# Attention and gated MLP on one core: a floor on the size of a dense phase, maxima closed by reductions, a normalization on ACT, and output tiles fetched two ahead

## The chip, the cores and the metric

The kernel runs on one core of one Trainium2 chip. The metric is device time in microseconds, the median of several runs. The kernel before has a median of 2049.7 us over three runs (2048.86 to 2051.69). Engines: PE is the matrix engine (PEld its weight load), DVE the vector engine, ACT the scalar engine, POOL GpSimd; SP issues nearly all DMAs.

## The reference

Input x has S = 2048 rows of D = 512 values. It is layer-normalized once, and two branches of the result are added to x:

```python
xn = layernorm(x)                                        # 2048 x 512
q, k, v = split(xn @ wqkv)                               # 32 heads of 16
A = concat_heads(softmax(q @ k.T / 4) @ v) @ wo          # attention
z = gelu(xn @ w_in)                                      # 2048 x 1792
z1, z2 = z[:, :896], layernorm(z[:, 896:])
g = w_sp @ z2 + b_sp[:, None]                            # 2048 x 2048 by 2048 x 896
out = x + A + (z1 * g) @ w_out
```

## The kernel before

The order of the instructions of each engine is written out by hand: a Python loop, which runs when the kernel is built, emits everything, and each engine then executes its own list in order. Two kinds of work share PE.

The first is attention. Two heads at a time (16 pairs), 4 chunks of 512 queries, 16 key tiles: 1024 steps. A step of the scores (`scores`, line 800) is a pair of matmuls into a PSUM tile `st`, which ACT turns into exp values `pf` (`exp`, line 814). The row maxima that the softmax subtracts come from another product of the same size: `max_mm` (line 556) writes a tile `mx`, `max_red` (line 566) reduces it on DVE. `st` and `mx` take turns in one ring of three PSUM tiles. `pv` (line 788) multiplies two steps of `pf` with v into `o`, eight small matmuls. `max_mm` runs 27 steps ahead of `scores`. After each 16 steps `max_fin` (line 574) closes a chunk: it negates the maxima, splits them into a rounded part and the rest (lines 581, 583, 584), transposes them (586), and two sets of DMAs bring them as additional rows into the operand of the scores.

The second is dense work, a `queue` of generators: the q and k projections (`qk_rest`), the second half of the first MLP product with its GELU and normalization (`z2_all`, `z2_norm`), its first half (`z1_all`), the product along the sequence (`spatial`), the last MLP product (`mlp_out`), the attention's output (`attn_out`). Each float32 product is three matmuls of rounded parts (`mm3`, line 164), called a triple here; after each triple the generator yields its cost in ns (650, or 570 in `z2_all`). An accumulator (`dpsum`, one PSUM bank) takes 4 triples in `qk`, `z2p`, `z1p` and `ao`, 16 in `sp`, 7 in `mo`.

The loop (line 832) goes by halves; two halves are a round of three steps. The first half emits st, mx, st and one or two `pv`; the second emits mx, st, mx and then a dense phase. A budget, `credit`, grows each round by three steps' share of the dense work still to do, spread to step 925 (`DENSE`). The phase goes on while the budget is positive:

```python
while credit > 0 and queue and not pause and not drain:
```

`drain` ends a phase at an accumulator's last triple (a yield with a fraction), because the bank must be emptied first; a yield that is not positive sets a pause, used at the start of a stage (-3) and where weights are missing (-1.5).

Weights are loaded by `prepare` (line 194): DMA into one of three raw buffers, then POOL rounds and splits them (`end`). As soon as `end` has been emitted the weight stands in the dictionary that its user polls. Work of POOL is timed by a model of its own: `gps` adds a cost to `pool[0]`, `clock()` is 2.7 us per half, and `pool_done` lets a generator wait until the model says that POOL has finished. `z2_norm` runs beside the dense phases as a side generator: GELU on POOL and ACT, statistics on DVE, the inverse deviation on POOL (lines 362 to 368), the normalization on DVE (370), the split for the next product. `attn_out` fetches a tile's operands from DRAM with `fetch` one tile ahead (lines 662 to 669).

Of the kernel before, what the change touches and what calls it, by code (L numbers as in the profile page):

```python
# [39 lines left out]
def fused_block(ctx, tc, x, wqkv, wo, w_in, w_spT, b_sp, w_out, out):  # L40
# [56 lines left out]

    steady = []
    side = []

    def raw(t):
        return t.bitcast(F32) if t.dtype == F32R else t
# [47 lines left out]
    def hilo(nm):  # L150
        return big.tile([P, 2, 512], F32R, tag="hilo", name=nm, bufs=3)

    def dpsum(nm, tag="d"):
        return ps.tile([P, 512], F32, tag=tag, name=nm, bufs=1)

    def spsum(nm):
# [37 lines left out]
    def prepare(out, loads, freed=None):  # L194


        loads, flight = list(loads), []
        while loads or flight:
            if flight and now[0] >= flight[0][0]:
                _, k, l = flight.pop(0)  # L200
                out[k] = end(l)
                rawfree.append(pool[0])
            if loads and len(rawfree) > 0 and clock() >= rawfree[0] and (freed is None or freed and now[0] >= freed[0]):
                rawfree.pop(0)
                if freed:
                    freed.pop(0)
                k, *a = loads.pop(0)
                flight.append((now[0] + 2, k, begin(*a)))
            yield
# [72 lines left out]
    def qk_group(m, g, w, tags=("d",)):  # L282
        for a in range(2):
            if now[0] < -2 and m:
                tags = ("d", "o")
            acc = dpsum(f"qk{m}_{a}_{g}", tags[a % len(tags)])
            for c in range(ND):
                t = xnT[g, c]
                mm3(acc, w[a][:, 0, c * P:(c + 1) * P], w[a][:, 1, c * P:(c + 1) * P], t[:, 0, :], t[:, 1, :], c == 0, c == ND - 1)
                yield 650 + 0.5 * (c == ND - 1)  # L290
            if m == 0:
                run(qk_split(m, g, a, acc))
                yield 0
                continue
            raw_ = t512(f"qr{m}_{a}_{g}")
            act(raw_, acc, AF.Copy, 512)
            side.append(qk_split(m, g, a, raw_))
            yield 0
# [43 lines left out]
    def z2_norm(t, z):  # L342


        z = z[:, :FH]
        u = piece(f"z2u{t}").bitcast(F32).rearrange("p a b -> p (a b)")[:, :FH]
        yield
        gelu_in(z, u, FH)
        yield from pool_done()
        act(u, u, AF.Tanh, FH, scale=GC)  # L350
        act(u, u, AF.Identity, FH, bias=1.0)
        yield
        gps(0.0024 * FH).tensor_mul(z, z, u)
        yield from pool_done()
        st = sm.tile([P, 2, 6], F32, tag="zst", name=f"zst{t}", bufs=2)
        mv = sm.tile([P, 2], F32, tag="zmv", name=f"zmv{t}", bufs=2)
        rs = sm.tile([P, 3], F32, tag="zrs", name=f"zrs{t}", bufs=2)
        for j in range(2):
            dve(448).bn_stats(st[:, j, :], z[:, j * 448:(j + 1) * 448])
        dve(12).bn_aggr(mv, st)  # L360
        yield
        gps(0.2).tensor_scalar(rs[:, 0:1], mv[:, 1:2], 1.0, 4 * EPS, ALU.mult, ALU.add)
        gps(0.6).tensor_tensor(rs[:, 1:2], rs[:, 0:1], mhalf, ALU.pow)

        gps(0.3).tensor_mul(rs[:, 2:3], rs[:, 1:2], rs[:, 1:2])
        gps(0.3).tensor_mul(rs[:, 2:3], rs[:, 2:3], rs[:, 0:1])
        gps(0.3).tensor_scalar(rs[:, 2:3], rs[:, 2:3], -0.5, 1.5, ALU.mult, ALU.add)
        gps(0.3).tensor_mul(rs[:, 1:2], rs[:, 1:2], rs[:, 2:3])
        yield from pool_done()
        dve(FH, 2).tensor_scalar(z, z, mv[:, 0:1], rs[:, 1:2], ALU.subtract, ALU.mult)  # L370
        for j, (lo, w) in enumerate(((0, 512), (512, 384))):
            yield
            hl = hilo(f"z2hl{t}_{j}")
            act(hl[:, 0, :w], z[:, lo:lo + w], AF.Copy, w)
            yield
            gps(0.0025 * w).tensor_sub(hl[:, 1, :w], z[:, lo:lo + w], hl[:, 0, :w].bitcast(F32))
            for a in range(2):
                store(z2scr[:, lo // P:(lo + w) // P, a, t, :], hl[:, a, :w].rearrange("p (f q) -> p f q", q=P), 1 + a)

    def z2_all():  # L380
# [11 lines left out]
        for t in range(NT):  # L392
# [4 lines left out]
                bg.append(prepare(w1, [(f, f"w1_{f}", w_in[:, f * P:(f + 1) * P], D, ND) for f in range(NF)]))  # L397
            z = piece(f"z2_{t}").bitcast(F32).rearrange("p a b -> p (a b)")
            for j in range(2):
                acc = dpsum(f"z2p{t}_{j}")  # L400
                for c in range(ND):
                    sl = slice(c * P, (c + 1) * P)
                    mm3(acc[:, :448], xt[:, 0, sl], xt[:, 1, sl], ws[c, j][:, 0, :448], ws[c, j][:, 1, :448], c == 0, c == ND - 1)
                    yield 570 + 0.5 * (c == ND - 1)
                act(z[:, j * 448:(j + 1) * 448], acc[:, :448], AF.Copy, 448)
                if j:
                    side.append(z2_norm(t, z))
                yield 0
# [12 lines left out]
    def z1_all():  # L421
        fetch_xnT(0)
        yield -2.5
        for g in range(NG):
            for f in range(NF):
# [3 lines left out]
                    fetch_xnT(g + 1, 2)  # L429
                while f not in w1:  # L430
                    yield -1.5
                acc = dpsum(f"z1p{f}_{g}")
                w = w1[f]
                for c in range(ND):
                    t = xnT[g, c]
# [11 lines left out]
    def spatial():  # L447
# [18 lines left out]
        order = [(g, f) for g in range(NG) for f in range(NF)]  # L466
        for n, (g, f) in enumerate(order):
            load_z1(g, f)
            acc = dpsum(f"sp{g}_{f}")
            nc.tensor.matmul(acc, onesr, brow, start=True, stop=False)  # L470
            if f == NF - 1 and g + 1 < NG:
                load_b(g + 1)
# [28 lines left out]
    def mlp_out():  # L501
# [14 lines left out]
        for t in range(NT):  # L516
# [2 lines left out]
                nxt = load(t + 1)  # L519
            if t == NT - 3:  # L520
                bg.append(prepare(wo_, [(g, f"wo{g}", wo[g * P:(g + 1) * P, :], 512) for g in range(4)]))
            acc = dpsum(f"mo{t}")
            for f in range(NF):
                h, sl = hp[f // 4], slice((f % 4) * P, (f % 4 + 1) * P)
                mm3(acc, h[:, 0, sl], h[:, 1, sl], wout[f][:, 0, :], wout[f][:, 1, :], f == 0, f == NF - 1)
# [48 lines left out]
    def max_fin(i):  # L574
# [2 lines left out]
            return  # L577
        g = i // 16
        p, c = divmod(g, 4)
        mn = at.tile([P, 2, 4], F32, tag="mn", name=f"mn{g}", bufs=1)  # L580
        nc.vector.tensor_reduce(mn, mmax.pop(g), AX.X, ALU.max, negate=True)
        mr = mrow[:, 0:16].rearrange("p (j a t) -> p j a t", j=2, a=2)
        nc.vector.tensor_copy(mr[:, :, 0, :], mn)
        nc.vector.tensor_sub(mr[:, :, 1, :], mn, mr[:, :, 0, :].bitcast(F32))
        ms = at.tile([P, 32], F32, tag="ms", name=f"ms{g}", bufs=2)
        nc.vector.transpose(ms, mrow.bitcast(F32))
        load["D"] += 0.6
# [50 lines left out]
    def attn_out():  # L638
# [18 lines left out]
        for j in range(2):  # L657
# [1 line left out]
            gps(0.2).tensor_add(ones[:, 0, j * DH:(j + 1) * DH], a, b)  # L659
            a, b = (ident[:, 64 * j + 32 * r + DH:64 * j + 32 * r + DH + 1].to_broadcast([P, DH]) for r in range(2))  # L660
            gps(0.2).tensor_add(ones[:, 0, (2 + j) * DH:(3 + j) * DH], a, b)
        nxt = fetch(0)
        yield -3
        while len(wo_) < 4:
            yield -1.5
        for t in range(NT):
            op = nxt
            if t + 1 < NT:
                nxt = fetch(t + 1)
            while t // 4 not in lasthl:  # L670
                yield -1
            acc = dpsum(f"ao{t}")
            for g in groups:
                mm3(acc, op[:, 0, g, :], op[:, 1, g, :], wo_[g][:, 0, :], wo_[g][:, 1, :], g == 0, False)
                yield 650
# [55 lines left out]
    with tc.manual_schedule(engines=engines):  # L731
# [76 lines left out]
        N = len(order)  # L808
        sts, full = {}, {}
        credit = 0.0  # L810
        ready = rounds = 0
        ended = []

        def exp(n):
            pf = at.tile([P, 1024], F32, tag="pf", name=f"pf{n}", bufs=PF)
# [16 lines left out]
        for half in range(-2 * LEAD // 3, 2 * (N // 3 + 4)):  # L832
# [60 lines left out]
            if urgent and between and not drain and "ones" in sel:  # L893
                queue.insert(0, urgent.pop(0))
                pause = 0
            while credit > 0 and queue and not pause and not drain:
                cost = next(queue[0], None)
                if cost is None:
                    queue.pop(0)
                elif cost <= 0:  # L900
                    pause = -cost
                else:
                    drain = between = cost % 1 > 0
                    credit -= cost
                    todo -= cost
        while queue or urgent or bg or late or turn:
            now[0] += 1
            flush()
# [35 lines left out]
```

## Time and profile before

| | |
|---|---|
| median of three runs | 2049.7 us |
| the profiled execution's own time | 2054.62 us |
| its span, first to last instruction | 2052.8 us |
| PE busy | 1991.7 us, 97% |
| DVE busy | 1457.4 us, 71% |
| ACT busy | 1219.3 us, 59% |
| POOL busy | 517.0 us, 25% |
| mean granted clock of PE | 0.990 |

The rows of the trace that the prediction uses stand in a section below. In a row of the timeline the columns are start, duration, engine, line, operation, output and inputs, and in brackets how long the engine had been idle before it and what released it.

### The profile page before, as it was taken

Reading aid. Unit: us, or ns where it says so; the run is one execution under the profiler, and the core shown is the slowest. Engines: PE = TensorE matmul, PEld = TensorE weight load, DVE = VectorE, ACT = ScalarE, POOL = GpSimd, SP = SyncE. Lnnn points to the kernel's source line nnn. Section 1 sums busy time; section 2 is a strip of 40 time slices with the busy share of each in tenths; the row PEclk is TensorE's granted clock in tenths of the full one; section 3 lists DMA queues with packets and bytes.
Section 4 is the critical chain, followed back from the end, with each engine's and each line's share of the span. In section 5 each row is a group of like instructions: output and inputs, shape, how many; then the busy total and the mean of one; then the engine's idle time right before and its main releaser. Section 6 shows DMA issues by size and latency. Waiting matters only on the chain.

```text
span 2052.8 us, 30367 instructions
## 1 busy us (share of the span) xinstructions
PE 1991.7 (97%) x11548; PEld 1030.6 (50%) x11548; DVE 1457.4 (71%) x1614; ACT 1219.3 (59%) x1396; POOL 517.0 (25%) x560
## 2 busy tenths in 40 slices
PE   7999999899999999999999999999999999999998
PEld 6764454454444445454444455545554454454442
DVE  5377788878777767776777777777777767766773
ACT  4346677676666655555555655555566655555555
POOL 2203267677344620005011320005001200011100
PEclk9999999999999999999999999999999999999999
DMA  9586253354434545354454745255364635353322
GB/s 323 189 317 200 93 137 106 92 127 141 129 105 131 153 152 135 99 150 155 113 143 138 203 142 133 91 129 181 108 161 142 172 123 154 97 167 102 103 80 96
DMA packets 233850, 293.05 MB, mean 143 GB/s; under 512 B 34656, under 2 KB 134688, under 8 KB 230824
## 3 DMA queue, kind: packets, MB, share of 16 engines
q1 hardware_dynamic: 229480, 281.07, 46.8%
q0 software_dynamic: 4224, 10.04, 1.3%
q8 instruction: 91, 1.49, 0.3%
q14 instruction: 55, 0.45, 0.1%
HBM read 189.06 MB, written 101.98 MB: 142 GB/s over the span
## 4 chain that ended last, share of the span: by engine, by line
PE 86%; DVE 8%; DMA 3%; ACT 1%; issue 1%; SPq 1%; POOL 0%; DVEq 0%; ACTq 0%; POOLq 0%
PE o L798 22%; PE mx L564 15%; PE st L805 14%; PE sp L165 6%; DVE mm L572 6%; PE sp L166 5%; PE sp L167 5%; PE mo L165 2%; PE z1p L165 1%; PE qk L165 1%; PE z2p L165 1%; PE mo L166 1%; PE mo L167 1%; PE qk L166 1%; PE qk L167 1%; PE z1p L166 1%
## 5 line engine op out<-in xcount | busy, mean ns | idle before, releaser
L572 DVE TENSOR_REDUCE mm<-mx 128x2 f32<-128x1024 f32 x1024 | 1218.2, 1221 | 498.8 <-PE mx L564 497.7
L57 ACT ACTIVATE pf<-st 128x1024 f32<-128x1024 f32 x1024 | 1017.7, 1024 | 716.8 <-PE st L805 696.4
L798 PE MATMUL o<-pf,vall 128*32 128x512 f32 x4096 | 518.0, 607 | 0.0
L805 PE MATMUL st<-qst,kst 50*128 50x512 f32 x2048 | 450.3, 437 | 25.9 <-DVE mm L572 23.5
L564 PE MATMUL mx<-kst,qst 48*128 48x512 f32 x2048 | 459.1, 446 | 7.2 <-DVE mm L572 3.3
L564 PEld LDWEIGHTS mx<-kst,qst 48*128 48x128 f32 x2048 | 193.0, 186 | 354.2 <-ACT pf L57 288.7
L805 PEld LDWEIGHTS st<-qst,kst 50*128 50x128 f32 x2048 | 193.5, 186 | 195.5 <-DVE mm L572 91.9
L798 PEld LDWEIGHTS o<-pf,vall 128*32 128x32 f32 x4096 | 99.0, 109 | 221.7 <-issue 220.0
L165 PE MATMUL sp<-wsp,zs 128*128 128x512 f32 x448 | 191.1, 427 | 1.4 <-POOL wsp L190 1.4
L166 PE MATMUL sp<-wsp,zs 128*128 128x512 f32 x448 | 176.4, 394 | 0.0
L167 PE MATMUL sp<-wsp,zs 128*128 128x512 f32 x448 | 175.7, 392 | 0.6 <-POOL wsp L191 0.6
L165 PEld LDWEIGHTS sp<-wsp,zs 128*128 128x128 f32 x448 | 83.9, 187 | 56.2 <-issue 40.1
L190 POOL CAST wsp<-wsp_0r 128x512 fp32r<-128x512 f32 x4 | 2.5, 612 | 370.9 <-DMA wsp_0r<-in_w_spT 370.9
L167 PEld LDWEIGHTS sp<-wsp,zs 128*128 128x128 f32 x448 | 84.1, 188 | 20.5 <-POOL wsp L191 1.1
L166 PEld LDWEIGHTS sp<-wsp,zs 128*128 128x128 f32 x448 | 84.3, 188 | 13.3
L615 POOL TENSOR_TENSOR ob<-ob 128x512 f32<-128x512 f32 (+1 forms) x16 | 20.5, 1283 | 255.4 <-DMA ob<-escr 255.4
L620 POOL TENSOR_TENSOR ob<-ob 128x512 f32<-128x512 f32 (+1 forms) x16 | 20.6, 1288 | 162.4 <-DMA ob<-rscr 104.4
L165 PE MATMUL z2p<-w,xt 128*128 128x448 f32 x128 | 52.1, 407 | 0.0
L165 PE MATMUL mo<-wout,hp 128*128 128x512 f32 x112 | 48.5, 433 | 0.0
L190 POOL CAST wo<-wo0r 128x512 fp32r<-128x512 f32 x1 | 0.6, 612 | 188.8 <-DMA wo0r<-in_wo 188.8
L167 PE MATMUL z2p<-w,xt 128*128 128x448 f32 x128 | 47.6, 372 | 0.0
L166 PE MATMUL z2p<-w,xt 128*128 128x448 f32 x128 | 47.6, 372 | 0.0
(371 smaller groups left out, 1918.8 us busy)
## 6 DMA issues: line engine op xcount, KB each, us to landing
zs<-z2scr SPq DMA_DIRECT2D x112, 512.0 KB
escr<-e SPq DMA_DIRECT2D x60, 256.0 KB
hscr<-hhl SPq DMA_DIRECT2D x28, 512.0 KB
qst<-qscr SPq DMA_DIRECT2D x30, 384.0 KB
kst<-kscr SPq DMA_DIRECT2D x30, 384.0 KB
xscr<-xnT POOLq DMA_DIRECT2D x16, 512.0 KB, 5.9
qscr<-qkhl SPq DMA_DIRECT2D x16, 512.0 KB
kscr<-qkhl SPq DMA_DIRECT2D x16, 512.0 KB
```

The lines of the kernel that those rows point to most:

```text
L57: return nc.scalar.activation(out, in_, func, **kw)
L165: nc.tensor.matmul(acc, lh, rh, start=first, stop=False)
L166: nc.tensor.matmul(acc, ll, rh, start=False, stop=False)
L167: nc.tensor.matmul(acc, lh, rl, start=False, stop=last)
L190: gps(0.6).tensor_copy(t[:, 0, :n], rw[:, :n])
L564: nc.tensor.matmul(acc[:, j, :], qst[p % 2][rows, tt * P:(tt + 1) * P], kst[p % 2][rows, kc * 512:(kc + 1) * 512], start=True, stop=True)
L572: dve(1024).tensor_reduce(mmax[i // 16][:, :, t, kc], mstep.pop(i), AX.X, ALU.max)
L615: gps(1.3).tensor_add(both[rows, 0, :], both[rows, 0, :], both[rows, 1, :])
L620: gps(1.3).tensor_mul(both[rows, 0, :], both[rows, 0, :], both[rows, 2, :])
L798: nc.tensor.matmul(acc[cols:cols + VW, :], vpack(kt - 1 + r, 2 * p + j), pf[:, j * 512:(j + 1) * 512], start=(kt == 1), stop=(kt == NT - 1))
L805: nc.tensor.matmul(st[:, j, :], kst[p % 2][rows, kt * P:(kt + 1) * P], qst[p % 2][rows, c * 512:(c + 1) * 512], start=True, stop=True)
```

## The change

Four edits.

1. `dpsum` notes in `left` how many triples its accumulator takes, and each triple counts it down. The phase's condition becomes `go()`: the first triple needs a positive budget; the second is always taken; a third and further ones need a positive budget while more than two triples are left in the accumulator; with two left they need more than 650; with one left the triple is taken.
2. In `prepare` a weight enters the user's dictionary only when the model clock has passed POOL's end of its split (`made`).
3. `max_fin` closes a chunk with four `tensor_reduce`: the rounded negative maximum, the exact negative maximum, the rounded positive one, and the sum of the last two, which is the rest. Before, it was a `tensor_reduce`, a `tensor_copy` and a `tensor_sub`.
4. `z2_norm` works out -mean/deviation with two more small operations on POOL and normalizes on ACT (`Identity` with scale and bias) in place of DVE's `tensor_scalar`; `attn_out` fetches two tiles ahead in place of one.

```diff
@@ -97,6 +97,7 @@
     steady = []
     side = []
+    left = [0]
     def raw(t):
         return t.bitcast(F32) if t.dtype == F32R else t
@@ -150,7 +151,8 @@
     def hilo(nm):
         return big.tile([P, 2, 512], F32R, tag="hilo", name=nm, bufs=3)
-    def dpsum(nm, tag="d"):
+    def dpsum(nm, tag="d", n=1):
+        left[0] = n
         return ps.tile([P, 512], F32, tag=tag, name=nm, bufs=1)
     def spsum(nm):
@@ -194,11 +196,15 @@
     def prepare(out, loads, freed=None):
-        loads, flight = list(loads), []
-        while loads or flight:
+        loads, flight, made = list(loads), [], []
+        while loads or flight or made:
+            if made and clock() >= made[0][0]:
+                _, k, t = made.pop(0)
+                out[k] = t
             if flight and now[0] >= flight[0][0]:
                 _, k, l = flight.pop(0)
-                out[k] = end(l)
+                t = end(l)
+                made.append((pool[0], k, t))
                 rawfree.append(pool[0])
             if loads and len(rawfree) > 0 and clock() >= rawfree[0] and (freed is None or freed and now[0] >= freed[0]):
                 rawfree.pop(0)
@@ -283,7 +289,7 @@
         for a in range(2):
             if now[0] < -2 and m:
                 tags = ("d", "o")
-            acc = dpsum(f"qk{m}_{a}_{g}", tags[a % len(tags)])
+            acc = dpsum(f"qk{m}_{a}_{g}", tags[a % len(tags)], ND)
             for c in range(ND):
                 t = xnT[g, c]
                 mm3(acc, w[a][:, 0, c * P:(c + 1) * P], w[a][:, 1, c * P:(c + 1) * P], t[:, 0, :], t[:, 1, :], c == 0, c == ND - 1)
@@ -366,8 +372,10 @@
         gps(0.3).tensor_mul(rs[:, 2:3], rs[:, 2:3], rs[:, 0:1])
         gps(0.3).tensor_scalar(rs[:, 2:3], rs[:, 2:3], -0.5, 1.5, ALU.mult, ALU.add)
         gps(0.3).tensor_mul(rs[:, 1:2], rs[:, 1:2], rs[:, 2:3])
+        gps(0.3).tensor_mul(rs[:, 2:3], mv[:, 0:1], rs[:, 1:2])
+        gps(0.3).tensor_scalar(rs[:, 2:3], rs[:, 2:3], -1.0, 0.0, ALU.mult, ALU.add)
         yield from pool_done()
-        dve(FH, 2).tensor_scalar(z, z, mv[:, 0:1], rs[:, 1:2], ALU.subtract, ALU.mult)
+        act(z, z, AF.Identity, FH, bias=rs[:, 2:3], scale=rs[:, 1:2])
         for j, (lo, w) in enumerate(((0, 512), (512, 384))):
             yield
             hl = hilo(f"z2hl{t}_{j}")
@@ -397,7 +405,7 @@
                 bg.append(prepare(w1, [(f, f"w1_{f}", w_in[:, f * P:(f + 1) * P], D, ND) for f in range(NF)]))
             z = piece(f"z2_{t}").bitcast(F32).rearrange("p a b -> p (a b)")
             for j in range(2):
-                acc = dpsum(f"z2p{t}_{j}")
+                acc = dpsum(f"z2p{t}_{j}", n=ND)
                 for c in range(ND):
                     sl = slice(c * P, (c + 1) * P)
                     mm3(acc[:, :448], xt[:, 0, sl], xt[:, 1, sl], ws[c, j][:, 0, :448], ws[c, j][:, 1, :448], c == 0, c == ND - 1)
@@ -429,7 +437,7 @@
                     fetch_xnT(g + 1, 2)
                 while f not in w1:
                     yield -1.5
-                acc = dpsum(f"z1p{f}_{g}")
+                acc = dpsum(f"z1p{f}_{g}", n=ND)
                 w = w1[f]
                 for c in range(ND):
                     t = xnT[g, c]
@@ -466,7 +474,7 @@
         order = [(g, f) for g in range(NG) for f in range(NF)]
         for n, (g, f) in enumerate(order):
             load_z1(g, f)
-            acc = dpsum(f"sp{g}_{f}")
+            acc = dpsum(f"sp{g}_{f}", n=NT)
             nc.tensor.matmul(acc, onesr, brow, start=True, stop=False)
             if f == NF - 1 and g + 1 < NG:
                 load_b(g + 1)
@@ -519,7 +527,7 @@
                 nxt = load(t + 1)
             if t == NT - 3:
                 bg.append(prepare(wo_, [(g, f"wo{g}", wo[g * P:(g + 1) * P, :], 512) for g in range(4)]))
-            acc = dpsum(f"mo{t}")
+            acc = dpsum(f"mo{t}", n=NF)
             for f in range(NF):
                 h, sl = hp[f // 4], slice((f % 4) * P, (f % 4 + 1) * P)
                 mm3(acc, h[:, 0, sl], h[:, 1, sl], wout[f][:, 0, :], wout[f][:, 1, :], f == 0, f == NF - 1)
@@ -577,11 +585,16 @@
             return
         g = i // 16
         p, c = divmod(g, 4)
-        mn = at.tile([P, 2, 4], F32, tag="mn", name=f"mn{g}", bufs=1)
-        nc.vector.tensor_reduce(mn, mmax.pop(g), AX.X, ALU.max, negate=True)
+        mm = mmax.pop(g)
+        mn = at.tile([P, 2, 4, 2], F32, tag="mn", name=f"mn{g}", bufs=1)
         mr = mrow[:, 0:16].rearrange("p (j a t) -> p j a t", j=2, a=2)
-        nc.vector.tensor_copy(mr[:, :, 0, :], mn)
-        nc.vector.tensor_sub(mr[:, :, 1, :], mn, mr[:, :, 0, :].bitcast(F32))
+        nc.vector.tensor_reduce(mr[:, :, 0, :], mm, AX.X, ALU.max, negate=True)
+        nc.vector.tensor_reduce(mn[:, :, :, 0], mm, AX.X, ALU.max, negate=True)
+        nc.vector.tensor_reduce(mn.bitcast(F32R)[:, :, :, 1], mm, AX.X, ALU.max)
+        with nc.allow_low_precision(reason="the second of two parts, of which the first is exact"):
+            nc.vector.tensor_reduce(mr[:, :, 1, :], mn, AX.X, ALU.add)
         ms = at.tile([P, 32], F32, tag="ms", name=f"ms{g}", bufs=2)
         nc.vector.transpose(ms, mrow.bitcast(F32))
         load["D"] += 0.6
@@ -659,17 +672,17 @@
             gps(0.2).tensor_add(ones[:, 0, j * DH:(j + 1) * DH], a, b)
             a, b = (ident[:, 64 * j + 32 * r + DH:64 * j + 32 * r + DH + 1].to_broadcast([P, DH]) for r in range(2))
             gps(0.2).tensor_add(ones[:, 0, (2 + j) * DH:(3 + j) * DH], a, b)
-        nxt = fetch(0)
+        nxt = [fetch(0), fetch(1)]
         yield -3
         while len(wo_) < 4:
             yield -1.5
         for t in range(NT):
-            op = nxt
-            if t + 1 < NT:
-                nxt = fetch(t + 1)
+            op = nxt.pop(0)
+            if t + 2 < NT:
+                nxt.append(fetch(t + 2))
             while t // 4 not in lasthl:
                 yield -1
-            acc = dpsum(f"ao{t}")
+            acc = dpsum(f"ao{t}", n=4)
             for g in groups:
                 mm3(acc, op[:, 0, g, :], op[:, 1, g, :], wo_[g][:, 0, :], wo_[g][:, 1, :], g == 0, False)
                 yield 650
@@ -808,8 +821,16 @@
         N = len(order)
         sts, full = {}, {}
         credit = 0.0
+        took = 0
         ready = rounds = 0
         ended = []
+        def go():
+            if took == 0 or left[0] > 2 and took > 1:
+                return credit > 0
+            return left[0] == 1 or took == 1 or credit > 650
         def exp(n):
             pf = at.tile([P, 1024], F32, tag="pf", name=f"pf{n}", bufs=PF)
@@ -893,7 +914,8 @@
             if urgent and between and not drain and "ones" in sel:
                 queue.insert(0, urgent.pop(0))
                 pause = 0
-            while credit > 0 and queue and not pause and not drain:
+            took = 0
+            while queue and not pause and not drain and go():
                 cost = next(queue[0], None)
                 if cost is None:
                     queue.pop(0)
@@ -903,6 +925,8 @@
                     drain = between = cost % 1 > 0
                     credit -= cost
                     todo -= cost
+                    left[0] -= 1
+                    took += 1
         while queue or urgent or bg or late or turn:
             now[0] += 1
             flush()
```

## Rows read from the trace of the kernel before

**Rows 1.** The page, busy us and share of the span by engine.
```profile
PE 1991.7 (97%) x11548; PEld 1030.6 (50%) x11548; DVE 1457.4 (71%) x1614; ACT 1219.3 (59%) x1396; POOL 517.0 (25%) x560
```
**Rows 2.** Waits of PE's matmuls: us in total, times, longest.
```profile
PE st L805 <- DVE mm L572: 23.5, 56, 3.0
...
PE ao L165 <- DMA op<-oscr: 3.0, 2, 1.5
...
PE sp L165 <- POOL wsp L190: 1.4, 1, 1.4
```
**Rows 3.** Timeline, PE behind a phase of one triple.
```profile
513.65 0.50 PE L805 MATMUL st<-qst,kst 50*128 50x512 f32 x2
...
514.59 0.50 PE L805 MATMUL st<-qst,kst 50*128 50x512 f32 x2 [0.20 <-DVE mm L572]
```
**Rows 4.** Timeline, DVE in the same stretch.
```profile
512.19 3.48 DVE L572 TENSOR_REDUCE mm<-mx 128x2 f32<-128x1024 f32 x3
```
**Rows 5.** Windows of four rounds: start:end, us, busy us by engine, clock, DMA.
```profile
513.65:520.77 7.12, 6.92 (x41) 3.56 (x40) 5.06 (x5) 4.02 (x6) 3.96 (x4) 1.00 0.94 265
563.44:570.04 6.60, 6.60 (x41) 3.56 (x40) 5.03 (x9) 3.56 (x4) 2.77 (x3) 1.00 0.62 219
1043.49:1050.77 7.28, 7.07 (x42) 3.75 (x41) 5.97 (x8) 3.62 (x4) 1.28 (x1) 1.00 0.35 110
1241.47:1248.28 6.81, 6.81 (x42) 3.75 (x41) 5.54 (x10) 3.48 (x4) 0.00 (x0) 1.00 0.44 119
```
**Rows 6.** Timeline, PE, behind the first and the last of the 35 phases.
```profile
159.54 0.50 PE L805 MATMUL st<-qst,kst 50*128 50x512 f32 x2 [0.27 <-DVE mm L572]
...
1955.66 0.50 PE L805 MATMUL st<-qst,kst 50*128 50x512 f32 x2 [0.21 <-DVE mm L572]
```
**Rows 7.** Lines 581, 583, 584: duration ns min/median/max, first and last start, forms.
```profile
L581 DVE TENSOR_REDUCE mn<-mm x64: 169/177/190, 122.2 to 2001.3; 128x8 f32<-128x32 f32 x64
...
L583 DVE CAST mrow<-mn x64: 170/171/1857, 122.4 to 2001.5; 128x8 fp32r<-128x8 f32 x64
...
L584 DVE TENSOR_TENSOR mrow<-mn,mrow x64: 166/168/2000, 122.6 to 2001.7; 128x8 fp32r<-128x8 f32 x64
```
**Rows 8.** Timeline, one close of a chunk: POOL, DVE, then PE.
```profile
405.52 2.09 POOL L353 TENSOR_TENSOR z<-z,z2u 128x896 f32<-128x896 f32 x1
...
405.64 2.00 DVE L584 TENSOR_TENSOR mrow<-mn,mrow 128x8 fp32r<-128x8 f32 x1
...
409.05 0.80 PE L805 MATMUL st<-qst,kst 50*128 50x512 f32 x2 [3.02 <-DVE mm L572]
```
**Rows 9.** Windows of two rounds of the z2 stage.
```profile
374.05:383.49 9.44, 6.70 (x33) 2.13 (x33) 6.00 (x9) 5.27 (x6) 4.36 (x8) 0.82 0.40 114
...
409.05:419.12 10.07, 10.07 (x32) 5.61 (x33) 5.92 (x7) 5.18 (x6) 1.36 (x6) 0.50 0.55 139
```
**Rows 10.** Line 370; ACT on tiles of 896, by lines; the z2 stage (windows).
```profile
L370 DVE TENSOR_SCALAR z<-z,zmv,zrs x16: 705/1265/2461, 249.2 to 506.3; 128x896 f32<-128x896 f32 x16
...
L57 ACT ACTIVATE z2u<-z2u 128x896 f32<-128x896 f32 x29 | 27.7, 954 | 0.4
...
209.00:464.00 255.00, 241.84 (x1417) 127.51 (x1416) 202.04 (x218) 181.46 (x226) 158.04 (x170) 0.97 0.40 107
```
**Rows 11.** Timeline, POOL's last small operation of a z2 tile, DVE's normalization.
```profile
247.76 0.19 POOL L368 TENSOR_TENSOR zrs<-zrs 128x1 f32<-128x1 f32 x1
...
249.18 0.89 DVE L370 TENSOR_SCALAR z<-z,zmv,zrs 128x896 f32<-128x896 f32 x1
```
**Rows 12.** Timeline, PE at two tiles of the attention's output.
```profile
1892.53 0.47 PE L165 MATMUL ao<-wo,op 128*128 128x512 f32 x1 [1.45 <-DMA op<-oscr]
...
1920.25 0.47 PE L165 MATMUL ao<-wo,op 128*128 128x512 f32 x1 [1.55 <-DMA op<-oscr]
```
**Rows 13.** Windows: a round with no dense phase; start of the output stage.
```profile
707.03:711.41 4.38, 3.13 (x22) 1.13 (x22) 3.49 (x4) 3.71 (x6) 4.22 (x6) 1.00 0.66 152
...
1872.00:1881.00 9.00, 8.65 (x30) 5.10 (x32) 3.79 (x4) 3.89 (x5) 1.28 (x1) 0.62 0.64 189
```

## The prediction

> **What bounds the kernel now.** I read the page first: PE is busy 97% of the span, every other engine at most 71% [rows 1]. So only two things can help: less PE work, of which the change takes none away, or fewer holes and slow stretches of PE. Next the waits of PE's own matmuls: the largest entry, 23.5 us in 56 waits, is a score tile that waits for a DVE reduction; two waits for the output's operands come to 3.0 us [rows 2]. Then the timeline of PE, round by round. From the first score matmul of one round to that of the next, a round's length depends on two things alone in undisturbed places: whether it holds one or two emissions of `pv` (8 or 16 small matmuls), and the number of triples. With 16, an undisturbed round takes 6.60 us with 4 triples of z1, and 6.81 with 4 of sp and the bias matmul (second and fourth of [rows 5]). Of the 332 rounds from 149 to 1999 us, those that are longer than their like are of four kinds, and they follow here.
>
> **Phases of one triple (edit 1).** 41 rounds hold one triple: 10 in z2p, 9 in z1p, 9 in sp, 5 in mo, 4 each in qk and ao. The reason is the mechanism of the budget: 3 triples leave it below zero, the fourth of an accumulator comes a round later, alone, and then the accumulator ends the phase. In the ring of three PSUM tiles the second score tile of the next round takes the place of the second mx of the round before. DVE needs 3.48 us for its three reductions, from 512.19 to 515.67 in the case shown, the last of them for a later tile [rows 4]; with one triple between, PE is back at 513.65, and its second score tile starts only at 514.59, released by DVE [rows 3]. The round behind a single is then 7.12 against 6.60 in z1p and 7.28 against 6.81 in sp, with the same 16 small matmuls and the same triples [rows 5]: 0.52 and 0.47, taken as 0.5. Rounds behind a phase of two show no such excess, and the single rounds themselves are not longer than their one triple asks. Of the 41, four are followed by a round with no phase at the end of a stage, one by the last pair's sums and one by the disturbed round of the next part. The other 35 (the first and the last in [rows 6]) give 35 x 0.5 = 17 us.
>
> Does `go()` remove them? In accumulators of 4 the phase now has 4 triples where the budget is over 1950 (1790 in z2p, at 570 each) at its start, otherwise 2. Income is about 1850 per round, more than the 1300 of two triples, so no round goes empty for that, and the work done per round stays. In sp and mo the third triple goes by the old rule, a last one is always taken. A single is left only where a pause cuts a phase. Bounds: 12 (a third stay) to 20 (the 23.5 of [rows 2] less the 3.0 of [rows 8], which is of another kind). I take 17.
>
> **Chunks of maxima (edit 3).** Lines 583 and 584 take 0.17 us by the median and up to 1.86 and 2.00; line 581, a reduction, never more than 0.19 in 64 chunks [rows 7]. The long ones coincide with two-input operations of POOL: in the case shown POOL starts at 405.52 for 2.09, DVE's subtraction starts at 405.64 and ends with it, and the cast before it, 1.86 long, ended so with the POOL operation before. PE stands 3.02 us for the reductions behind, and restarts with matmuls of 0.80 in place of 0.50 [rows 8]: the granted clock is 0.50, the lower level of 1.2 GHz, for the whole round that follows, 10.07 us of PE work that would be about half at 2.4 GHz [rows 9]. Two places are like this, both in the z2 stage. The round at 374.05 is 9.44 us long with 6.70 of PE busy, so 2.7 idle, and its mean clock is 0.82, so 0.18 x 9.44 = 1.7 lost to the clock [rows 9]: 4.4. The idle 3.02 of [rows 8] ends the round before 409.05, and of the 10.07 behind it at most half, 5.0, is the clock's; I take 4.5, since other waits would have shown again. Sum 4.4 + 3.0 + 4.5 = 11.9.
>
> All four closing operations are now of the kind of line 581. The Trainium skill, SBUF — State Buffer, "Who interferes with whom", says it as a rule: a copy, a cast or a `tensor_scalar` can need the port pair that DVE shares with GpSimd, a subtraction with two SBUF inputs contends with its reads, a `tensor_reduce` never does. The trace agrees [rows 7]; by this rule each close stays under 1 us wherever POOL is, and all of the 11.9 could go. The Trainium skill also speaks against the edit: VectorE: DVE Perf Modes, "Rules for kernel authors", calls `tensor_reduce` the slowest DVE operation, always at the single rate, to be restructured on a hot path. By that page the edit would lose a little in each of 64 closes; the reduction of 32 values takes 7 ns more than the cast of 8 by the medians [rows 7], 64 x 4 x 7 ns = 2 us of DVE in all.
>
> The cost: one operation more per chunk, 0.18 plus a start of 0.03, 64 x 0.21 = 13 us of DVE work. DVE is idle 29% of the span [rows 1], so most of it is covered; where a round is short and holds a close, up to 0.2 shows. I charge 1 in all, with 0 and 13 as ends. In the two bad rounds DVE still has statistics and a close, so I count 11 of the 11.9 as gained (8 to 12).
>
> **Normalization on ACT (edit 4).** 16 operations of line 370 leave DVE, 0.71 to 2.46 us each, median 1.27 [rows 10], also stretched by POOL. ACT gets 16 of 0.95, by its other operations of 896 elements, 15 us; in the z2 stage (255 us) ACT goes from 181 to 196 busy, DVE from 202 to about 181 [rows 10]. POOL gets 16 x 2 operations of 0.19 plus gaps of 0.08, 9 us, behind which nothing of PE waits. What is queued behind the new ACT operation is the next exp, and behind that a score tile: if POOL is late, PE stands. Before, DVE found POOL's values ready by 1.2 us or more in each of the 16 tiles; the narrowest is that of [rows 11], and the two new operations need 0.56 of it. So: no new wait. The effect on PE is that of a few half microseconds in z2p rounds: between 4 gained and 3 lost, taken as 1 gained.
>
> **Output tiles two ahead (edit 4) and stage starts.** PE waits 1.45 and 1.55 for a tile of `op` [rows 12]: 3 us, which go if the fetch is one tile earlier, since a tile's four triples and what is between take over 5 us. More pieces of the ring of 20 are in use, at most 17 by my count (8 output tiles, 3 operands, 4 weights, 2 for the last pair), so no fetch waits for a piece. Each stage starts with rounds of no phase, 4.38 us with PE busy 3.13 in one, so 1.2 lost, and a slow clock behind them, 0.62 over 9 us at the output stage, 3.4 lost [rows 13]. They stay, as the pause of 3 stays; where the single ahead of them goes, the hole is smaller: 2 gained (0 to 8, four such stretches).
>
> **Weights flagged later (edit 2).** A weight is seen one half later, so a phase may be put off; on the other hand PE no longer stands for POOL's split. It did for 1.4 us in one wait [rows 2]. With 8 changes of weights (4 stages and the 4 columns of w_sp), I take 0, from 1 gained to 10 lost (8 rounds without a phase at 1.2, as that of [rows 13]).
>
> **Sum.** 17 + 11 + 1 + 3 + 2 - 1 = 33 us, of 2054.6 for the profiled execution: 2021.6. That execution is 4.9 us above the median of the runs, so the same gain from 2049.7 gives 2016.7: 2017 us.
>
> **Rivals.** (a) The loss behind singles isn't cured but moved: DVE's reductions set the pace over two rounds, and phases of two in place of three and one give the same waits in smaller parts. For it: DVE is at 71% [rows 1], and its three reductions alone are 3.5 us of each round [rows 4]. Against: rounds behind two triples show no excess. Time: 17 less gained, 2034. (b) The chunk closes still collide, or another DVE operation (the GELU's, line 340) meets POOL instead, and the low clock falls elsewhere: 11 less gained, 2028. (c) The weights' flag makes stages start late: 16 rounds without a phase at 1.2, 19 us: 2036. (d) Slower: ACT's normalization waits for POOL at the head of ACT's list, the exp behind it is late, and PE stands in each of the 16 z2 tiles as in the round at 374, 2.7 us [rows 9]; from 33/16 = 2.1 us per tile on the whole gain is gone; at 2.7 the time is 2017 + 43 = 2060. Against it stands the slack of [rows 11].
>
> **How the numbers follow.** The forecast has 0.70, (a) 0.10, (b) 0.11, (c) 0.04, (d) 0.05. All but (d) are faster by more than 0.2% (4 us, about what can be told from no change); for what I have not thought of I move 0.07 away: faster 0.88, same 0.06, slower 0.06. The low end takes nearly all bounds at their best, 20 + 12 + 4 + 3 + 5 = 44: 2005 or so. The high end takes in (a), (b) and (c): 2038.
>
> **What would show it.** In the trace after: no dense phase of one triple inside a stage, and the wait of `st` for `mm` under 6 us. The closing reductions all near 0.18 us. No stretch at the low clock between 370 and 420. No wait of `ao` for `op`. ACT never waiting for `zrs`. Wrong: PE's waits for DVE still near 20 us, a new entry of ACT waiting for POOL, or more rounds without a phase than six.

## The result, and the profile after

The changed kernel takes 2019.55 us (median of 4, 2015.84 to 2020.96), the kernel before 2049.82 beside it. The ratio is 0.9844 with a 95% interval of 0.9825 to 0.9862. In a later series it was 0.9829 (0.9815 to 0.9844). That is 32 to 35 us; 33 were forecast, and 2017.

The page of the changed kernel, busy us and share of the span (2016.4 us), to be compared with [rows 1]:

```profile
PE 1976.3 (98%) x11548; PEld 1027.4 (51%) x11548; DVE 1427.1 (71%) x1662; ACT 1229.9 (61%) x1412; POOL 518.2 (26%) x592
```

PE has the same 11548 matmuls and is 15 us less busy; the rest of the 36 us of span was idle. Read window by window, the time at a granted clock of 0.50 fell from 42.8 to 24.8 us, and half of that difference, 9, is about what the clock gave back (an estimate). The rounds behind a single triple also counted as busier, 6.92 us against 6.60 in [rows 5]. The waits of PE's matmuls, to be compared with [rows 2]:

```profile
PE st L818 <- DVE mm L580: 8.0, 18, 0.9
PE z1p L167 <- DMA xnT__4621<-xscr: 2.7, 1, 2.7
...
PE ao L167 <- DMA op<-oscr: 0.3, 1, 0.3
```

The score tile's wait for a reduction fell from 23.5 us in 56 places to 8.0 in 18, and the output's operands from 3.0 to 0.3. No round holds a single triple any more: the rounds of z1 now hold 4 or 2. Windows of three rounds, columns as in [rows 5]:

```profile
552.89:559.49 6.60, 6.60 (x42) 3.57 (x42) 4.59 (x5) 3.45 (x4) 3.32 (x4) 1.00 0.55 141
...
381.68:388.02 6.34, 5.59 (x35) 2.51 (x35) 3.45 (x4) 6.05 (x7) 5.37 (x5) 1.00 0.21 59
...
238.01:243.09 5.08, 5.08 (x37) 2.45 (x36) 3.00 (x3) 4.35 (x6) 2.21 (x2) 1.00 0.13 51
```

The first is the 4-triple round behind a phase of two: 6.60, PE without a hole, where the round behind a single took 7.12 in [rows 5]. The other two are rounds of two z2 triples with 16 small matmuls; behind a phase of four such a round is 5.08, behind a phase of two it can be 6.34. This is new, and is taken up below.

The four operations that close a chunk (minimum, median, maximum ns; the first of 64 and one case in order of time), against [rows 7] and [rows 8]:

```profile
L593 DVE TENSOR_REDUCE mrow<-mm x64: 174/177/189, 120.8 to 1965.3; 128x8 fp32r<-128x32 f32 x64
...
455.60 0.17 DVE L593 TENSOR_REDUCE mrow<-mm 128x8 fp32r<-128x32 f32 x1
455.70 0.18 DVE L594 TENSOR_REDUCE mn<-mm 128x8 f32<-128x32 f32 x1
455.79 0.18 DVE L595 TENSOR_REDUCE mn<-mm 128x8 fp32r<-128x32 f32 x1
456.00 0.17 DVE L597 TENSOR_REDUCE mrow<-mn 128x8 fp32r<-128x16 f32 x1
456.20 0.21 DVE L599 STREAM_TRANSPOSE ms<-mrow 128x32 f32<-128x32 f32 x1
```

Not one is stretched (the maxima of the other three are 180, 180 and 171 ns), and the first three, which don't depend on each other, start 0.10 apart. From the first start to the transposition it is 0.60 us for four operations; three took 0.62 at the first close of the kernel before, where nothing stretched them.

One stretch got no better, the start of z1. Timeline of PE, window of the round, and window of the slow clock:

```profile
465.31 0.47 PE L167 MATMUL z1p<-xnT__4621,w 128*128 128x512 f32 x1 [2.68 <-DMA xnT__4621<-xscr]
...
465.79:472.62 6.83, 6.39 (x17) 3.35 (x16) 0.00 (x0) 0.30 (x1) 4.93 (x4) 0.50 0.72 237
458.25:471.49 13.24, 9.83 (x41) 4.45 (x42) 4.57 (x4) 4.91 (x6) 11.88 (x14) 0.78 0.84 269
```

PE waits 2.68 us for a transfer and then works 6.83 us at a granted clock of 0.50, the 1.2 GHz level. This differs from run to run. In another profile of the same kernel, whose run took 2013.19 us, the only such stretch here is 3.41 us long and lies ahead of the start, at 456.12; behind the waits for the same transfers (0.91, 0.33 and 0.68) the clock is full. The kernel before had its own stretch there, 3.4 us from 470.4.

### The profile page after: what moved, and what is told of

Its sections match the earlier page's. It is cut to its first block, busy times and chain, and to the rows that moved or that the text cites. A ratio compares the mean times of both kernels' runs of the same rounds, so it can differ in the third digit from the quotient of the medians.

```text
span 2016.4 us, 30429 instructions
## 1 busy us (share of the span) xinstructions
PE 1976.3 (98%) x11548; PEld 1027.4 (51%) x11548; DVE 1427.1 (71%) x1662; ACT 1229.9 (61%) x1412; POOL 518.2 (26%) x592
## 5 line engine op out<-in xcount | busy, mean ns | idle before, releaser
L57 ACT ACTIVATE pf<-st 128x1024 f32<-128x1024 f32 x1024 | 1015.0, 1024 | 670.8 <-PE st L818 653.9
L811 PE MATMUL o<-pf,vall 128*32 128x512 f32 x4096 | 512.8, 602 | 0.0
```

Source lines behind the costliest of these rows:

```text
L57: return nc.scalar.activation(out, in_, func, **kw)
L811: nc.tensor.matmul(acc[cols:cols + VW, :], vpack(kt - 1 + r, 2 * p + j), pf[:, j * 512:(j + 1) * 512], start=(kt == 1), stop=(kt == NT - 1))
```

## Experiments

All were timed over five rounds, beside the kernel before on the same chip; so each has its own ratio, and differences between series go by the ratios. Two readings run through the expectations. By the additive theory each edit is worth its own term of the sum, whatever the others do; by coupling, two edits remove parts of the same stall, so their gains don't add up.

**Edit 1 alone.** The kernel before with `left`, `took` and `go()`:

```diff
-            while credit > 0 and queue and not pause and not drain:
+            took = 0
+            while queue and not pause and not drain and go():
```

> The kernel before with the floor of two triples alone (edit 1). Additive theory: the singles are worth 17 us by themselves, so about 2033 against 2050, and the stalls at the chunk closes near 374 and 405 with their low clock stay. Rival (coupling): both bad closes of the kernel before lie in rounds of a single triple; with two triples there PE has cover for the late reductions, so the closes no longer show and this edit alone gives 25 us or more, 2025 or less. Rival (a) of the prediction, the loss is only moved: under 8 us.

Measured: 2027.93, ratio 0.9893 (0.9878 to 0.9907), 22 us. That lies between the additive theory and coupling. One bad place of the z2 stage had gone and one was left, with the low clock behind it. DVE in that place:

```profile
362.25 2.00 DVE L372 TENSOR_SCALAR z<-z,zmv,zrs 128x896 f32<-128x896 f32 x1
364.17 1.21 DVE L574 TENSOR_REDUCE mm<-mx 128x2 f32<-128x1024 f32 x1
365.30 0.17 DVE L585 TENSOR_REDUCE mn<-mm 128x8 f32<-128x32 f32 x1
365.51 1.76 DVE L587 CAST mrow<-mn 128x8 fp32r<-128x8 f32 x1
367.31 1.21 DVE L588 TENSOR_TENSOR mrow<-mn,mrow 128x8 fp32r<-128x8 f32 x1
```

and PE behind it:

```profile
371.18 0.79 PE L566 MATMUL mx<-kst,qst 48*128 48x512 f32 x2 [2.48 <-DVE mm L574]
```

From 370.91 to 377.73 the granted clock is 0.50. The stall is a pile: a stretched normalization and a stretched close in one round. Two triples don't cover 5 us of them, and three didn't either. The same pile in the kernel before, DVE and then PE:

```profile
367.49 2.17 DVE L370 TENSOR_SCALAR z<-z,zmv,zrs 128x896 f32<-128x896 f32 x1
370.92 1.75 DVE L583 CAST mrow<-mn 128x8 fp32r<-128x8 f32 x1
372.71 1.22 DVE L584 TENSOR_TENSOR mrow<-mn,mrow 128x8 fp32r<-128x8 f32 x1
...
372.03 0.47 PE L165 MATMUL z2p<-w,xt 128*128 128x448 f32 x1
376.60 0.49 PE L564 MATMUL mx<-kst,qst 48*128 48x512 f32 x2 [2.04 <-DVE mm L572]
382.56 0.47 PE L165 MATMUL z2p<-w,xt 128*128 128x448 f32 x1
```

That both bad closes lie in rounds of a single triple, as the expectation has it, holds for the one at 405 alone. Here the close lies in a round of three triples, whose first matmul is the one at 372.03, and the single triple of the next round, at 382.56, comes behind the stall. The other bad place went with this edit, but not because two triples cover a long close there: the same close, now at 398.39, is hardly stretched (cast 0.46 and subtraction 0.17 us).

**Edit 3 alone.** The kernel before with the four reductions:

```diff
-        nc.vector.tensor_reduce(mn, mmax.pop(g), AX.X, ALU.max, negate=True)
...
-        nc.vector.tensor_copy(mr[:, :, 0, :], mn)
-        nc.vector.tensor_sub(mr[:, :, 1, :], mn, mr[:, :, 0, :].bitcast(F32))
+        nc.vector.tensor_reduce(mr[:, :, 0, :], mm, AX.X, ALU.max, negate=True)
+        nc.vector.tensor_reduce(mn[:, :, :, 0], mm, AX.X, ALU.max, negate=True)
+        nc.vector.tensor_reduce(mn.bitcast(F32R)[:, :, :, 1], mm, AX.X, ALU.max)
...
+            nc.vector.tensor_reduce(mr[:, :, 1, :], mn, AX.X, ALU.add)
```

> The kernel before with the chunk closed by four reductions alone (edit 3). Additive theory: 11 us, about 2039; the waits of st for mm stay near 17 us, since singles stay. Coupling: the same here, 8 to 12 us, since singles are still there to expose the closes. Rival (b), the closes still collide: 0 to 2 us.

Measured: 2040.76, ratio 0.9953 (0.9938 to 0.9968), 10 us, as both theories had it; that the closes still collide is refuted. From 370 to 420 the granted clock is 1.00. At the first bad place the normalization is still 2.16 us long, and behind it PE waits 0.25 us: without the stretched close the pile is too small to matter.

**Edits 1 and 3 together**, both diffs above:

> Edits 1 and 3 together on the kernel before, without the flag, the ACT normalization and the earlier fetch. Additive theory: 28 us, 2022. Coupling: about as much as edit 1 alone, plus 2 to 5: 2020 to 2025. In both the two waits of ao for op stay.

Measured: 2023.29, ratio 0.9874 (0.9858 to 0.9890), 26 us. Apart they are worth 22 and 10. So some 6 us are counted by both, though the intervals are wide against that. It fits the rows: of the 11.9 us that the prediction reads from [rows 8] and [rows 9], 7.5 belong to the place that edit 1 removes too, and the 4.4 of the place that it leaves are about what edit 3 adds on top of it, 4 (an estimate).

**Edit 1 undone in the changed kernel**, the first diff the other way:

> The changed kernel with the budget's old condition (edit 1 undone). Additive theory: 17 us slower than the changed kernel, about 2036, about 41 phases of one triple again and st waiting for mm about 20 us. Rival (a): under 8 us slower.

Measured: 2029.20, ratio 0.9901 (0.9886 to 0.9916), 12 to 15 us slower than the changed kernel in its two series; the additive 17 is just too much, rival (a)'s 8 too little. 40 phases of one triple are back, and with them the wait for DVE:

```profile
PE st L818 <- DVE mm L580: 19.4, 51, 0.9
```

**Is it DVE that a single phase waits for?** The same kernel, with each reduction of maxima over half its keys:

```diff
-            while queue and not pause and not drain and go():
+            while credit > 0 and queue and not pause and not drain:
...
-        dve(1024).tensor_reduce(mmax[i // 16][:, :, t, kc], mstep.pop(i), AX.X, ALU.max)
+        dve(1024).tensor_reduce(mmax[i // 16][:, :, t, kc], mstep.pop(i)[:, :, :256], AX.X, ALU.max)
```

> The budget's old condition, so some 40 phases of one triple, but each reduction of maxima reads 256 of its 512 keys (the maxima of the other half are left out of what softmax subtracts), so DVE's three reductions take about half of 3.5 us. Theory (a round behind a single waits for DVE's third reduction): the excess of 0.47 us of these rounds goes, and with it all of the 10 to 14 us that the old condition cost, so at most 2018. Rival (the excess belongs to PE itself, to the change between the forms of matmul or to the short phase): the excess stays near 0.4 and the time near 2029.

Measured: 1999.34, ratio 0.9764 (0.9751 to 0.9777). Windows of a single z1 round and the 4-triple round behind it, first with whole reductions, then with halved ones:

```profile
514.01:517.93 3.92, 3.92 (x24) 1.66 (x23) 3.14 (x4) 3.13 (x4) 0.32 (x1) 1.00 0.12 44
517.93:525.06 7.13, 6.86 (x41) 3.57 (x41) 5.67 (x10) 3.90 (x5) 2.99 (x3) 1.00 0.16 54
```

```profile
504.53:508.45 3.92, 3.92 (x24) 1.61 (x23) 2.68 (x4) 3.11 (x4) 0.32 (x1) 1.00 0.18 67
508.45:515.06 6.61, 6.61 (x42) 3.57 (x41) 3.21 (x9) 3.83 (x5) 2.95 (x3) 1.00 0.15 46
```

The single rounds are equal. Behind them it is 7.13 with 0.27 of PE not busy, and 6.61 with no hole. Nothing of PE's list differs. So the excess is the wait for DVE, and neither the short phase itself nor the change between forms of matmul costs anything here. The time fell by 28 us, twice what the old condition costs, so halving takes away more than the waits behind singles: the time at a granted clock of 0.50 also falls from 20.4 to 5.2 us in the two profiles.

**The changed kernel with halved reductions**, the second half of that diff:

> The changed kernel with the same halved reductions (half of the maxima left out). In the changed kernel the second of two rounds with two z2 triples is still 0.5 to 0.7 us too long. Theory: these wait for DVE, so they shorten to the length of their like, and with the stage starts' waits for DVE 5 to 8 us go: about 2010. Rival: they wait for ACT, whose work is unchanged here: within 3 us of the changed kernel, and the halved reductions with singles then are no slower than this kernel.

Measured: 2002.15, ratio 0.9780 (0.9767 to 0.9793), 10 to 13 us faster than the changed kernel, more than either theory had, and yet the z2 rounds did not shorten, which is what the rival said of them: the round that was 6.34 is 6.32. Its window, ACT and PE in it:

```profile
375.57:381.89 6.32, 5.32 (x35) 2.44 (x34) 2.45 (x5) 6.03 (x7) 5.36 (x5) 1.00 0.21 60
...
374.39 1.95 ACT L57 ACTIVATE z2u<-z2u 128x896 f32<-128x896 f32 x2
376.25 2.83 ACT L57 ACTIVATE pf<-st 128x1024 f32<-128x1024 f32 x3
377.31 0.49 PE L818 MATMUL st<-qst,kst 50*128 50x512 f32 x2 [1.00 <-ACT pf L57]
```

ACT is busy 6.03 of 6.32 us. The exp stands behind two operations of the GELU, and the score tile behind the exp. These rounds belong to ACT. With halved reductions the singles (1999.34) are no slower than phases of two (2002.15): the floor of two is worth something only as long as DVE is late.

**Edit 3 undone in the changed kernel**, the second diff the other way:

> The changed kernel with the old close of a chunk (reduction, copy, subtraction; edit 3 undone). Additive theory: 11 us slower than the changed kernel, with DVE operations of the close up to 2 us long again in the z2 stage and low clock behind one or two of them. Coupling (phases of two triples cover a late close, and the normalization no longer lies on DVE): the operations are long again, but the time rises by 4 us or less.

Measured: 2014.37, ratio 0.9832 (0.9815 to 0.9848), beside 0.9829 for the changed kernel in the same series: nothing. The close is stretched again (minimum, median, maximum ns of the copy and the subtraction):

```profile
L593 DVE CAST mrow<-mn x64: 170/172/1156, 119.8 to 1966.6; 128x8 fp32r<-128x8 f32 x64
...
L594 DVE TENSOR_TENSOR mrow<-mn,mrow x64: 166/168/1206, 120.0 to 1966.8; 128x8 fp32r<-128x8 f32 x64
```

The longest, at 452.68, is 1.2 us instead of the 2.0 of [rows 7], and behind it PE waits twice as long as in the profile of this series' base. Here is the wait, and behind it the base's:

```profile
455.30 0.50 PE L815 MATMUL st<-qst,kst 50*128 50x512 f32 x2 [1.04 <-DVE mm L580]
...
454.75 0.50 PE L818 MATMUL st<-qst,kst 50*128 50x512 f32 x2 [0.49 <-DVE mm L580]
```

That is about half a microsecond. Coupling is right here as to the time. Its reason, that phases of two cover a late close, is not shown: no close of this kernel is as long as the two bad ones (at most 0.34 + 1.21 us, against 1.75 + 1.22 and 1.86 + 2.00), and the one close of 3 us among phases of two, in edit 1 alone, made PE stand.

**The changed kernel again**, the base of this series:

> The changed kernel once more, as the base for the three beside it: 2019.5 us or 0.985 of the kernel before.

Measured: 2014.72, ratio 0.9829 (0.9815 to 0.9844).

**Normalization back on DVE:**

```diff
-        gps(0.3).tensor_mul(rs[:, 2:3], mv[:, 0:1], rs[:, 1:2])
-        gps(0.3).tensor_scalar(rs[:, 2:3], rs[:, 2:3], -1.0, 0.0, ALU.mult, ALU.add)
         yield from pool_done()
-        act(z, z, AF.Identity, FH, bias=rs[:, 2:3], scale=rs[:, 1:2])
+        dve(FH, 2).tensor_scalar(z, z, mv[:, 0:1], rs[:, 1:2], ALU.subtract, ALU.mult)
```

> The changed kernel with the normalization of z2 back on DVE. Theory: 1 us slower, from 3 faster to 4 slower; DVE's operation 0.7 to 2.5 us long again. A rival by which the stretched DVE operations were the second half of the z2 stage's loss: 5 us or more slower.

Measured: 2020.15, ratio 0.9858 (0.9842 to 0.9875), 6 us slower than its base; the runs reach from 2014.26 to 2022.15, and the intervals overlap a little, so 6 is a best guess. The rival's mechanism stands once in the trace, where the changed kernel has in neither profile a wait of this size or a low clock:

```profile
284.02 2.38 DVE L376 TENSOR_SCALAR z<-z,zmv,zrs 128x896 f32<-128x896 f32 x1
287.60 0.51 PE L816 MATMUL st<-qst,kst 50*128 50x512 f32 x2 [1.51 <-DVE mm L578]
```

A stretched normalization makes PE stand, with no close beside it, and 3.4 us at the low clock follow: about 3 us in all (an estimate). But this is the profile of the fastest run, 1 us above the fastest of the base at the same granted clock of 0.997. The other three runs had 0.993 to 0.994, the base 0.995 to 0.998; where they lost it no trace shows. So the mechanism is the rival's, and the size stays open.

**Output tiles one ahead again:**

```diff
-        nxt = [fetch(0), fetch(1)]
+        nxt = fetch(0)
...
-            op = nxt.pop(0)
-            if t + 2 < NT:
-                nxt.append(fetch(t + 2))
+            op = nxt
+            if t + 1 < NT:
+                nxt = fetch(t + 1)
```

> The changed kernel with the output's tiles fetched one ahead again. Theory: 3 us slower, and PE waits for op once or twice for about 1.5 us; if the clock falls behind such a wait, up to 5 us. Rival: with other phases the transfer is in time anyway: within 1 us.

Measured: 2019.54, ratio 0.9851 (0.9837 to 0.9866), 4.5 us slower. The waits are back, 3.3 us more than in the base, and no low clock follows them in this profile:

```profile
PE ao L167 <- DMA op<-oscr: 3.6, 3, 2.2
```

**Weights entered at once (edit 2 undone):**

```diff
-        while loads or flight or made:
-            if made and clock() >= made[0][0]:
-                _, k, t = made.pop(0)
-                out[k] = t
+        while loads or flight:
...
-                t = end(l)
-                made.append((pool[0], k, t))
+                out[k] = end(l)
```

> The changed kernel with weights entering the dictionary as soon as their split is emitted (edit 2 undone). Theory: no difference, within 2 us of the changed kernel (0.983 to 0.984 of the kernel before). Rival: the flag is what took PE's waits for weights at the start of sp and the holes behind them away, then 3 us or more slower with PE waiting for wsp again.

Measured: 2018.61, ratio 0.9854 (0.9840 to 0.9867). Against the changed kernel's 0.9844 that is 2 us, against its 0.9829 it is 5, and there was no base in this series: inconclusive. PE waited once at the start of sp, for `zs`, and once for a weight, 0.62 us at 711.21, which it does in neither profile of the changed kernel. The first:

```profile
694.25 0.47 PE L167 MATMUL sp<-wsp,zs 128*128 128x512 f32 x1 [1.79 <-DMA zs<-z2scr]
```

**An attempt at the start of z1**, the first four fetches from ACT's queue:

```diff
-            move(xnT[g, c], xscr[g][c])
+            if on_act:
+                nc.scalar.dma_start(raw(xnT[g, c]), raw(xscr[g][c]))
+            else:
+                move(xnT[g, c], xscr[g][c])
```

> The changed kernel with the first four fetches of xnT for the z1 stage issued from ACT's queue in place of SP's, where they stand behind a store that waits 8 us for its data. Theory: PE's wait of 2.7 us at the start of z1 and the low clock behind it go, 3 to 6 us faster than the changed kernel. Rival: ACT's list delays them as much, or the DMA engines are the limit: within 2 us.

Measured: 2017.28, ratio 0.9845 (0.9832 to 0.9858): no gain. ACT's queue, ACT, and PE behind it:

```profile
464.11 0.33 ACTq L271 DMA_DIRECT2D xnT__4625<-xscr  x1
465.06 0.33 ACTq L271 DMA_DIRECT2D xnT__4627<-xscr  x1
465.43 1.94 ACT L57 ACTIVATE pf<-st 128x1024 f32<-128x1024 f32 x2 [6.68 <-DMA mscr<-ms]
466.51 0.80 PE L575 MATMUL mx<-kst,qst 48*128 48x512 f32 x2 [2.32 <-ACT pf L57]
```

The third and fourth fetch could be issued only at 464.11 and 465.06, and the exp behind them in the list stood with them, 6.68 us. PE no longer waits for the transfer but 2.32 us for that exp, with the low clock again. What held these two the profile does not name (`mscr` has nothing to do with them); that it was free pieces of the ring I argue, and have not shown.

## Why the prediction was right, and where its steps were not

The time, 2019.55 for 2017, and the sum, 32 to 35 for 33, were right, and so was the main mechanism. The terms were less so.

- **Singles, 17.** Mechanism right, and shown by the halved reductions: 7.13 becomes 6.61 with PE's list unchanged. Alone the edit is worth 22, on top of the others 12 to 15. The 17 lies between two things that I did not separate: alone, the edit also takes away the bad close at 405. The sign that I had set, waits of `st` for `mm` under 6 us, failed: 8.0 stay. And it gives something back: "rounds behind two triples show no excess" failed in the z2 stage, where two rounds of two triples in a row are now too short for ACT (6.34 where 5.08 would do). I had rival (a) look to DVE for that; it is ACT.
- **Closes, 11.** Alone 10, so the size was right against the kernel before. On top of the others nothing can be told (0.9832 to 0.9829). I took the stall at 376.60 for the close's own; it is a pile of a stretched normalization, a stretched copy and subtraction and the statistics, and shortening the close is one way to undo it. I also took the term to be independent of the phases; the place at 405 goes with edit 1 as well. With edits 1 and 4 in place no close is as long as these two, so nothing much is left for edit 3. That it comes out so is a matter of which POOL operation a close then meets, and I have not shown that it must.
- **Cost of the fourth operation, 1 (0 to 13).** Too high: 0.60 us from the first operation to the transposition. I priced four operations in a row, and three of them overlap, so the four take no longer than three did (0.62).
- **Normalization, 1.** Probably mis-sized: 6 by the medians, about 3 by the one place that the trace shows, 1 by the fastest runs. I saw the ACT cost (18.3 us measured for 15 forecast, 1.14 each) and DVE's relief, and priced the relief as a few half microseconds, where one stretched normalization can make PE stand 1.51 us and lose the clock behind it. That ACT would not wait for POOL was right: 0.4 us in 16 operations.

```profile
L57 ACT ACTIVATE z<-z,zrs 128x896 f32<-128x896 f32 x16 | 18.3, 1142 | 0.4 <-POOL zrs L376 0.4
```

- **Output tiles, 3.** 4.5 measured; the waits went from 3.0 to 0.3 us.
- **Stage starts, 2.** Not resolved. The start of the output stage has no slow clock like that of [rows 13] in either profile of the changed kernel, but in that with edit 3 undone it has, 6.9 us from 1844.5. Near the start of z1 it is 6.83 us in one profile and 3.41 in the other. So single runs differ by as much as the term.
- **Flag, 0.** 2 to 5 by ratios of different series, with one wait of 0.62 us for a weight in the trace, so open.

So the sum came out right in part by luck. Laid one on the other, edit 1 gave 22 (17 forecast), edit 3 on top of it 4 (10 forecast, with its cost), and the rest 6 to 9 (6 forecast): what the first gained too much, the second gained too little, because they share one loss.

## What to carry to other kernels

Where two engines hand tiles to each other through a short ring, look at the shortest stretch of work of the faster one, not at its mean: a phase shorter than the other engine's backlog costs about the difference, however idle that engine is on average. Halving the suspected operation in a copy of the kernel that is allowed to be incomplete tells in one run whose wait it is. Before adding up gains, ask whether two of them remove parts of the same stall; here edits worth 22 and 10 alone gave 26 together, and the second was worth nothing that could be measured at the end.

## What the runs showed that I had not expected

The same program differs by some microseconds from run to run (2013.19 to 2020.96 for the changed kernel), and the granted clock goes with it: 0.991 in a run of 2020.80, 0.998 in one of 2013.73. Between its two profiles the time at 0.50 is 24.8 and 11.8 us; half of the difference, 6.5, is an estimate of what it cost, and the spans differ by 5.7. So a term of 1 to 3 us can hardly be told from such runs without a trace.

And halving 1024 reductions, which PE's busy share of 98% would have called hidden, took 10 to 13 us off the changed kernel. In the traces PE's matmuls wait for these reductions 10.0 us in 20 places before and 2.5 in 6 after, and the time at 0.50 falls from 24.8 to 14.0 us, while one new wait of 3.7 us, for POOL, stands against that. The spans differ by 16.4 us, so a part has no wait of its own in the list.
